# Exponents of the last round written into the query slots, and three moves beside it, in a recurrent-memory attention kernel

## The chip, the cores and the metric

The kernel runs on one core of a Trainium2 chip. The metric is the device time of one execution in microseconds, and the median over several runs is quoted. Beside these runs one execution was recorded by the hardware profiler; its rows, in microseconds from the start of the span, are what the durations below come from.

## The reference

Four layers are applied in turn to x, 2048 tokens of 640 numbers: A, B, A, B, each on the layer norm of x and added to it.

```python
def _A_ref(x, mem0, Wq, Wk, Wv, Wo, seg_len):     # seg_len 32, M 8, H 32, Dh 192
    ...
    for s in range(n_seg):                        # 64 segments
        xs = x[:, s * seg_len:(s + 1) * seg_len, :].copy()
        h = jnp.concatenate([mem, xs], axis=1)
        q = jnp.einsum('btd,dhe->bhte', h, Wq)
        k = jnp.einsum('btd,dhe->bhte', h, Wk)
        v = jnp.einsum('btd,dhe->bhte', h, Wv)
        scores = jnp.einsum('bhqe,bhke->bhqk', q, k) * scale
        scores = jnp.where(mask[None, None], scores, -1000000000.0)
        p = _softmax(scores, axis=-1)
        o = jnp.einsum('bhqk,bhke->bhqe', p, v)
        o = jnp.einsum('bhte,hed->btd', o, Wo)
        mem = o[:, :M, :].copy()
        outs.append(o[:, M:, :])
    return jnp.concatenate(outs, axis=1)

x = x + _A_ref(_layernorm(x, axis=-1), A_mem0, A_Wq, A_Wk, A_Wv, A_Wo, A_seg_len)
x = x + _B_ref(_layernorm(x, axis=-1), B_wqkv, B_w_phi, B_wo)      # linear attention with softmax features
x = x + _A_ref(_layernorm(x, axis=-1), A_mem0, A_Wq, A_Wk, A_Wv, A_Wo, A_seg_len)
x = x + _B_ref(_layernorm(x, axis=-1), B_wqkv, B_w_phi, B_wo)
```

In an A layer the first eight output rows of one segment are the memory that the next segment starts from, so its 64 segments follow one another.

## The kernel before

**Stages.** An A layer has a preparation (`A_pre`), which computes what does not depend on the memory, and a chain (`A_chain`) over the 64 segments. The last eight tokens of a segment, called tails, don't depend on the memory: their keys, queries and values are made in the preparation, put into device memory (`kqb_d`, `vb_d`) and fetched back by POOL during the chain. The other 32 rows of a segment (8 of memory, 24 of tokens) are projected in the chain from `hT`. What the tails' queries attend to is kept in `otb_d` for all segments and multiplied by the output matrix only at the head of the following B layer (`post_steps`): there `fetch` brings 16 segments of it back, `spread` copies them into the order that the matmul takes (eight copies of 128x768, two for each round r; the letters v and s choose DVE or ACT), and `multiply` makes 48 pairs of matmuls into two PSUM tiles, `kv` and `ps_post`.

**One segment.** The 32 heads are taken in four rounds n = 0..3 of eight; L is 3, the last. Everything in the chain is issued in the order in which the program is written (`tc.manual_schedule()`), each engine taking its own instructions in that order. `QK` is one tile, of which `KT` holds the turned keys and `QT` the turned queries, eight slots of 80 columns each: columns 0 to 63 for rows of the chain, 64 to 79 for tails, which POOL copies in (L1069). In each round PE makes `ps_qk_q`, `ps_qk_k` and `ps_v` (L1092), ACT copies q and k out of PSUM into `raws` (L1107), and DVE transposes them into `QT` and `KT` (L1112). `scores` (L1129) multiplies them, ACT takes the exponents (L1218) into a tile `E`, of which there is one. `v_rows` copies the values out of `ps_v` into `Vp`, one half on ACT (L1119), the other on DVE (L1121). `attend` multiplies `E` with `Vp` for rows (L1142) and, as `attend_tails`, for tails (L1155). DVE takes the reciprocal of the sums of exponents (`weigh_rows`: L1162 in rounds 0 to 2, L1166, one for each G, in the last), ACT multiplies by it (`scaled`, L1172), DVE transposes the result (`turn`: L1285 in rounds 0 and 2, L1293 in 1 and 3), and `wo_round` (L1198) multiplies it by the output matrix, adding up over the rounds in a PSUM tile `ps_w`.

**The end of a segment.** The products of rounds 0 to 2 with the output matrix fill places where PE would wait. `outs` lists those not yet made as 14 steps of four matmuls, two steps of round 0, six of round 1, six of round 2, and `output_steps(k)` makes the next k. Two are made in round 2 (`STEPS[0]`), five after the last scores (`STEPS[1]`), the rest after the last `attend`. So in the last round, before the change, the order on the engines is:

- DVE: keys transposed (L1112, two halves), `turn` of round 2 (L1285), the values' half (L1121), `hx_transpose`, which fills `hT` of the next segment from its tokens (L1043), the reciprocals (L1166), `turn` of round 3 (L1293), and after the last `wo_round` the turn of `ps_w` (L1371) and the new memory rows (L1373).
- ACT: the scaling of round 2 (L1172, twice), the values' half (L1119), the exponents (L1218), the scaling of round 3 (L1172, twice).
- PE: values (L1092), scores (L1129), the tails of round 2 (L1155, they read the `E` of round 2), five output steps, `attend` (L1142, L1155), the rest of the output steps, `wo_round` of round 3, four matmuls into `ps_idle` (L1205), then the next segment's queries.

At the start of the next segment `keep_rows` (L1051, L1054) reads the finished `ps_w` on ACT and DVE. `ps_w` has two buffers, which take turns from segment to segment; the other chain pools have one bank for each tag. Behind the last segment come, in this order: the first `spread_tails` (before the last `wo_round`; two rounds on DVE, two on ACT, "vvss"), `weigh_tail` (L1178), `tail_rows` (L1183), the turn of it (L1187), `keep_rows`.

**PSUM at the border.** Pools hand out the eight banks in the order in which tiles first ask for them: `ps_qk_q` and `ps_qk_k` take the first two, `ps_w` the next two, then `ps_v`, `ps_s`, `ps_o`, `ps_t`. The B layer behind it takes three for `kv`, the fourth for its side tile, which is `ps_post` at first, and four for the rest.

Of the kernel before, what the change touches and what calls it, by code (L numbers as in the profile page):

```python
# [8 lines left out]
P = 128  # L9
BF16 = mybir.dt.bfloat16  # L10
# [16 lines left out]
VH = 194  # L27
# [1 line left out]
PACE = {("Q", 0): 0, ("K", 0): 1, ("V", 0): 3, ("Q", 1): 4, ("K", 1): 4, ("V", 1): 3, ("Q", 2): 1, ("K", 2): 0, ("V", 2): 0,  # L29
        ("Q", 3): 0, ("K", 3): 0}  # L30

STEPS = (2, 5)

LATE = 64512
ARENA = 201728
# [90 lines left out]
class Kernel:  # L126
# [876 lines left out]
    def A_chain(self, xn_dram, at_dram, li, load_slot, piece, late_wo, load_both, wo, low):  # L1003
# [3 lines left out]
        with tc.tile_pool(name=f"A{li}_ch", reuse_waits="tile", bufs=1) as sp, \  # L1007
# [126 lines left out]

            def attend(E, n):
                O = [pop.tile([P, 512], F32, name="ps_o", tag="o0")] * 2
                if n == NR - 1:
                    O[1] = pop.tile([P, 512], F32, name="ps_o1", tag="v")
                V = Vs[n % 2]
                for G in range(2) if n < NR - 1 else (1, 0):  # L1140
                    for h in range(4):
                        nc.tensor.matmul(O[G][32 * h:32 * h + 32, VH * G:VH * G + 193], lhsT=E[0:80, 80 * h + 32 * G:80 * h + 32 * G + 32],  # L1142
                                         rhs=V[0:80, VH * h:VH * h + 193], start=True, stop=True, tile_position=(0, 32 * h),
                                         skip_group_check=True)
                if n != 2:
                    attend_tails(E, n)
                return O

            def attend_tails(E, n):
                V = Vs[n % 2]  # L1150
                if n % 2 == 0:
                    pair[0] = pop.tile([P, 512], F32, name="ps_t", tag="o1")
                q, m = (48, 32) if n % 2 == 0 else (64, 16)
                for h in range(4):
                    nc.tensor.matmul(pair[0][32 * h:32 * h + m, 0:193], lhsT=E[0:80, 80 * h + q:80 * h + q + m],  # L1155
                                     rhs=V[0:80, VH * h:VH * h + 193], start=True, stop=True, tile_position=(0, 32 * h),
                                     skip_group_check=True)

# [54 lines left out]
            def weigh(E_before=None):  # L1213
                S = scores()
                if E_before is not None:
                    attend_tails(E_before, 2)
                E = sp.tile([P, 320], BF16, name="E", tag="E")
                nc.scalar.activation(out=E[0:80, 0:320], in_=S[0:80, 0:320], func=ACT.Exp, scale=scale)  # L1218
                return E

            turns = [(s, r) for s in range(NSEG) for r in rounds(s)]

# [17 lines left out]
            kqs.append(load_kqb(0, rounds(0)[3]))  # L1240
            load_rows(1)
            for s in range(NSEG):
                W = pop.tile([P, 512], F32, name="ps_w", tag="w", bufs=2)
                order = rounds(s)
                L = NR - 1

# [31 lines left out]
                def turn(n, osc):  # L1278
                    if n in (0, 2):
                        if n == 0:  # L1280
                            rows = ots[0].rearrange("p (c j) -> p c j", j=64)
                        else:
                            rows = raw_of["K"][:, 0:384].rearrange("p (c j) -> p c j", j=64)
                        OTs.append([rows[:, 3 * G:3 * G + 3, :] for G in range(2)])
                        nc.vector.transpose(out=rows, in_=osc.rearrange("p (c j) -> p c j", j=64))  # L1285
                        return
                    if n == L:
                        OTs.append([KT[:, 3 * G:3 * G + 3, 0:64] for G in range(2)])
                    else:
                        OTs.append([ots[1][:, 192 * G:192 * G + 192].rearrange("p (c j) -> p c j", j=64) for G in range(2)])  # L1290
                    parts = osc if n == L else [osc[:, 192 * G:192 * G + 192] for G in range(2)]
                    for v, part in list(zip(OTs[n], parts))[::-1 if n == L else 1]:
                        nc.vector.transpose(out=v, in_=part.rearrange("p (c j) -> p c j", j=64))  # L1293
# [8 lines left out]
                for n in range(L):  # L1302
# [33 lines left out]
                    osc = raw_of["Q"][:, 0:384]  # L1336
                    for G in range(2):
                        scaled(osc[:, 192 * G:192 * G + 192], O, rc, G, "s")
                    turn(n, osc)
                    v_rows(pv, n + 1, "sv")  # L1340
                    if n == 1:
                        otr = tail_rows(rct, "OTh")
                E = weigh(E)
# [13 lines left out]
                turn(L, oscs)  # L1357
                output_steps(len(outs))
                if s == NSEG - 1:
                    self.first_tails = tails, [self.spread_tails(0, tails[0], low, "vvss")]  # L1360
                if s + 1 < NSEG:
                    if s + 2 < NSEG:
                        load_rows(s + 2)
# [13 lines left out]
            store_tail(turn_tail(tail_rows(rct, "OTh"), ots[1][:, 0:192]), NSEG - 1, order[L])  # L1377
            keep_rows(W_done)
            store_rows(NSEG - 1)

    def keep_tails(self, tb, low):
        self.kept_tails.append(self.fetch_tails(tb, low))
# [8 lines left out]
    def spread_tails(self, tb, ot, low, engines="vsvs"):  # L1391
        o = 7680 + 12288 * (tb % 2)
        ow = low[:, o + 6144:o + 12288].rearrange("p (r j s x) -> p r j s x", r=4, j=6, x=16)
        for r in range(4):
            for b in range(2):
                at = 192 * (r // 2) + (0 if (r + b) % 2 else 16)
                o = ow[:, r, :, b:16:2, :]
                i = ot[:, b:16:2, at:at + 16]
                i = ap3(i, [list(i.ap[0]), [32, 6], *[list(d) for d in i.ap[1:]]])
                self.ev.copy(out=o, in_=i, eng=engines[r])  # L1400
        return ow
# [64 lines left out]
```

## Time and profile before

| | |
|---|---|
| median of 3 runs | 3265.13 us (3263.06 to 3274.89) |
| the profiled execution, its own time | 3262.61 us |
| its span | 3260.9 us |
| busy in it | PE 3093.0 us (95%), DVE 2207.3 (68%), ACT 1882.7 (58%), POOL 1411.0 (43%) |
| chain of layer 0, of layer 2 | about 175 to 1374 us, about 1813 to 3003 us |
| from the first L1166 of a segment to that of the next | 17.93 us at the least, 18.31 us in the median |
| idle of PE's weight loads before L1142, until ACT E L1218 | 45.6 us, 125 times |
| idle of ACT before L1218, until PE ps_t L1155 | 27.7 us, 128 times |
| idle of DVE before L1121, until ACT Vp L1119 | 23.0 us, 38 times |

The span is the recorded part of the execution; 1.7 us of the profiled execution's time lie around it. A row such as "L1121 DVE CAST Vp<-ps_v 64x384" is read as: line 1121, on DVE, a copy from the PSUM tile `ps_v` to `Vp`, of 64 partitions by 384 elements. In rows in order of time the first number is the start, the second the busy time, "xN" the number of instructions that the row merges, and square brackets hold the time that the engine idled before and what ended it. PEld is TensorE's weight load, PE the matmul.

### The profile page before, as it was taken

Reading aid. Unit: us, or ns where it says so; the run is one execution under the profiler, and the core shown is the slowest. Engines: PE = TensorE matmul, PEld = TensorE weight load, DVE = VectorE, ACT = ScalarE, POOL = GpSimd, SP = SyncE. Lnnn points to the kernel's source line nnn. Section 1 sums busy time; section 2 is a strip of 40 time slices with the busy share of each in tenths; the row PEclk is TensorE's granted clock in tenths of the full one; section 3 lists DMA queues with packets and bytes.
Section 4 is the critical chain, followed back from the end, with each engine's and each line's share of the span. In section 5 each row is a group of like instructions: output and inputs, shape, how many; then the busy total and the mean of one; then the engine's idle time right before and its main releaser. Section 6 shows DMA issues by size and latency. Waiting matters only on the chain.

```text
span 3260.9 us, 140891 instructions
## 1 busy us (share of the span) xinstructions
PE 3093.0 (95%) x59424; PEld 1976.8 (61%) x59730; DVE 2207.3 (68%) x5457; ACT 1882.7 (58%) x4481; POOL 1411.0 (43%) x2920
## 2 busy tenths in 40 slices
PE   9989999999999999899999899999999999998999
PEld 7756666666666666555367566666666666665553
DVE  5557777777777777656643577777777777776565
ACT  3346666666666666546433466666666666666453
POOL 3345555555555554430122355555555555554300
PEclk9999999999999999999999999999999999999999
DMA  8977777777777777840385777777777777778300
GB/s 301 379 274 261 239 252 250 237 256 248 244 260 235 258 248 244 278 155 1 112 318 192 241 239 264 245 256 242 254 253 244 260 238 253 249 245 284 129 1 33
DMA packets 325018, 747.58 MB, mean 229 GB/s; under 512 B 65818, under 2 KB 100274, under 8 KB 321314
## 3 DMA queue, kind: packets, MB, share of 16 engines
q1 hardware_dynamic: 254850, 638.55, 56.3%
q0 software_dynamic: 67616, 86.77, 9.6%
q10 hardware_dynamic: 1920, 13.24, 1.0%
q8 instruction: 469, 7.68, 1.0%
q14 instruction: 163, 1.34, 0.1%
HBM read 668.80 MB, written 77.03 MB: 229 GB/s over the span
## 4 chain that ended last, share of the span: by engine, by line
PE 75%; DMA 11%; DVE 7%; ACT 3%; issue 3%; POOL 0%; SPq 0%; PEld 0%; DVEq 0%; POOLq 0%; ACTq 0%
PE ps_qk_q L1092 12%; PE ps_qk_k L1092 12%; PE ps_v L1092 11%; PE ps_w L1198 10%; PE ps_pre L960 6%; PE ps_s L1129 5%; DMA arena<-in_A_Wv_dram 5%; DMA Vp<-vb 3%; PE ps_pre L989 3%; PE ps_o L1142 3%; PE kv L1421 2%; DMA arena<-wo_rows 2%; DVE raws L1371 2%; PE ps_wo L444 2%; DVE hT L1373 2%
## 5 line engine op out<-in xcount | busy, mean ns | idle before, releaser
L1092 PEld LDWEIGHTS <-hT 128*32 128x32 bf16 x30720 | 790.0, 97 | 422.7 <-issue 40.3
L1112 DVE STREAM_TRANSPOSE QK<-raws 128x512 bf16<-128x512 bf16 (+1 forms) x1152 | 730.4, 642 | 205.5 <-ACT raws L1107 171.4
L1092 PE MATMUL ps_qk_q<-arena,hT 128*32 128x384 bf16 x10240 | 508.5, 327 | 36.3 <-DVE hT L1373 30.4
L1092 PE MATMUL ps_qk_k<-arena,hT 128*32 128x384 bf16 x10240 | 510.0, 328 | 5.4 <-DMA arena<-in_A_Wk_dram 2.3
L1069 POOL COPY QK<-kqb 64x192 bf16<-64x192 bf16 x1024 | 350.4, 342 | 376.7 <-PE ps_s L1129 340.1
L1107 ACT ACTIVATE raws<-ps_qk_k 128x512 bf16<-128x512 f32 (+1 forms) x640 | 313.5, 510 | 253.5 <-PE ps_qk_k L1092 253.5
L1092 PE MATMUL ps_v<-arena,hT 128*32 128x384 bf16 x8192 | 436.0, 327 | 14.3 <-issue 6.8
L1073 POOL DMA_DIRECT2D Vp<-vb x512 | 257.6, 503 | 417.0 <-PE ps_t L1155 252.3
L1172 ACT ACTIVATE raws<-ps_o,rc 128x192 bf16<-128x192 f32 x1024 | 373.7, 420 | 109.8 <-DVE rc L1166 107.5
L1107 ACT ACTIVATE raws<-ps_qk_q 128x512 bf16<-128x512 f32 x512 | 305.7, 597 | 162.5 <-PE ps_qk_q L1092 151.2
L1062 POOL DMA_DIRECT2D kqb<-kqb x512 | 290.6, 568 | 70.9 <-POOL QK L1069 50.2
L1198 PE MATMUL ps_w<-arena,under 128*32 128x320 bf16 x6144 | 306.2, 300 | 11.9 <-issue 8.8
L1121 DVE CAST Vp<-ps_v 64x384 bf16<-64x384 f32 x512 | 286.3, 559 | 38.3 <-ACT Vp L1119 23.0
L1129 PEld LDWEIGHTS <-QK 128*80 128x80 bf16 x4096 | 195.5, 120 | 160.8 <-issue 156.6
L1119 ACT ACTIVATE Vp<-ps_v 64x384 bf16<-64x384 f32 x512 | 246.4, 481 | 55.6 <-PE ps_v L1092 54.8
L1129 PE MATMUL ps_s<-QK 128*80 128x80 bf16 x4096 | 256.4, 210 | 3.8 <-POOL QK L1069 2.8
L1218 ACT ACTIVATE E<-ps_s 80x320 bf16<-80x320 f32 x512 | 217.6, 425 | 30.7 <-PE ps_t L1155 27.7
L1051 ACT ACTIVATE wh<-ps_w 64x160 f32<-64x160 f32 x256 | 76.6, 299 | 266.1 <-DVE raws L1371 256.2
L1058 POOL DMA_DIRECT2D attn<-under x128 | 91.6, 716 | 294.2 <-DVE under L1054 291.3
L960 PEld LDWEIGHTS <-arena 128*128 128x128 bf16 x1920 | 188.4, 98 | 31.6 <-DVE next_xT L97 4.6
L97 DVE CAST arena<-ps_pre 128x512 bf16<-128x512 f32 (+1 forms) x160 | 102.2, 646 | 143.2 <-PE ps_pre L960 96.2
L1142 PE MATMUL ps_o<-Vp,E 80*32 80x193 bf16 x4096 | 179.9, 248 | 18.1 <-DMA Vp<-vb 7.4
(159 smaller groups left out, 4580.7 us busy)
## 6 DMA issues: line engine op xcount, KB each, us to landing
arena<-wo_rows SPq DMA_DIRECT2D x560, 320.0 KB, 5.5
arena<-in_A_Wq_dram SPq DMA_DIRECT2D x427, 384.0 KB, 4.2
arena<-in_A_Wk_dram SPq DMA_DIRECT2D x298, 384.0 KB, 4.7
arena<-in_A_Wv_dram SPq DMA_DIRECT2D x290, 384.0 KB, 6.0
kqb<-kqb POOLq DMA_DIRECT2D x512, 48.0 KB, 4.9
vb<-arena POOLq DMA_DIRECT2D x128, 97.0 KB, 6.1
Vp<-vb POOLq DMA_DIRECT2D x512, 24.2 KB, 4.0
kqb<-arena SPq DMA_DIRECT2D x8, 1536.0 KB, 9.7
```

The lines of the kernel that those rows point to most:

```text
L960: nc.tensor.matmul(ps[:, T * i:T * i + T], lhsT=w[b][:, P * c:P * c + P], rhs=xBT[:, b, :], start=(b == 0), stop=(b == KC - 1))
L1062: nc.gpsimd.dma_start(out=kqb[:], in_=self.kqb_d[r, :, s, :])
L1069: nc.gpsimd.tensor_copy(out=o, in_=kqb[h, :].rearrange("p (x c q) -> p x c q", c=3, q=16))
L1073: nc.gpsimd.dma_start(out=Vs[n % 2][64:80, :], in_=self.vb_d[s, r].rearrange("g t f -> (g t) f"))
L1092: last = nc.tensor.matmul(o, lhsT=hT[:, b, :], rhs=rhs, start=(i == 0), stop=(i == KC - 1), tile_position=(0, 32 * g), skip_group_check=True)
L1107: nc.scalar.activation(out=raw[:, c], in_=ps[:, c], func=ACT.Copy)
L1112: nc.vector.transpose(out=o, in_=i)
L1121: nc.vector.tensor_copy(out=o, in_=i)
L1129: nc.tensor.matmul(S[0:80, c0:c0 + 80], lhsT=KT[:, 4 * x + c, :], rhs=QT[:, 4 * x + c, :], start=(c % 2 == 0), stop=(c % 2 == 1), skip_gro ...
L1142: nc.tensor.matmul(O[G][32 * h:32 * h + 32, VH * G:VH * G + 193], lhsT=E[0:80, 80 * h + 32 * G:80 * h + 32 * G + 32], rhs=V[0:80, VH * h:V ...
L1172: nc.scalar.activation(out=out, in_=i, func=ACT.Copy, scale=rc[G])
L1198: step = nc.tensor.matmul(W[q:q + 32, 0:320], lhsT=OT[i // 6][:, i % 6 // 2, 32 * (i % 2):32 * (i % 2) + 32], rhs=rhs, start=(first and i ...
```

## The change

Four things change. The first three act in every segment of both chains or at their ends; the layers B are untouched.

1. `weigh` with an argument, which is the call of the last round, writes the exponents into `QT`, in two instructions: those of rows and the first 64 queries into slots 0 to 3, those of the last 16 queries of each head into slot 4. `attend` and `attend_tails` take a function that gives the columns. Rounds 0 to 2 use `E` as before.
2. In the third round (n = 2) `turn` is called behind `v_rows` instead of ahead of it, and `STEPS[1]` is 6 instead of 5, so that all steps ahead of the last `attend` are of round 1.
3. `ps_w` has one buffer instead of two.
4. The first `spread_tails` is split: its DVE half stays where it was, its ACT half is called at the very end of `A_chain`, behind `keep_rows` and `store_rows`.

```diff
-STEPS = (2, 5)
+STEPS = (2, 6)
...
-                        nc.tensor.matmul(O[G][32 * h:32 * h + 32, VH * G:VH * G + 193], lhsT=E[0:80, 80 * h + 32 * G:80 * h + 32 * G + 32],
+                        nc.tensor.matmul(O[G][32 * h:32 * h + 32, VH * G:VH * G + 193], lhsT=E(h, 32 * G, 32),
...
-                    nc.tensor.matmul(pair[0][32 * h:32 * h + m, 0:193], lhsT=E[0:80, 80 * h + q:80 * h + q + m],
+                    nc.tensor.matmul(pair[0][32 * h:32 * h + m, 0:193], lhsT=E(h, q, m),
...
                 S = scores()
                 if E_before is not None:
                     attend_tails(E_before, 2)
-                E = sp.tile([P, 320], BF16, name="E", tag="E")
-                nc.scalar.activation(out=E[0:80, 0:320], in_=S[0:80, 0:320], func=ACT.Exp, scale=scale)
-                return E
+                if E_before is None:
+                    E = sp.tile([P, 320], BF16, name="E", tag="E")
+                    nc.scalar.activation(out=E[0:80, 0:320], in_=S[0:80, 0:320], func=ACT.Exp, scale=scale)
+                    return lambda h, q, m: E[0:80, 80 * h + q:80 * h + q + m]
+                rows = S[0:80, 0:320].rearrange("p (h q) -> p h q", h=4)
+                nc.scalar.activation(out=QT[0:80, 0:4, 0:64], in_=rows[:, :, 0:64], func=ACT.Exp, scale=scale)
+                nc.scalar.activation(out=QT[0:80, 4, 0:64].rearrange("p (h q) -> p h q", h=4), in_=rows[:, :, 64:80],
+                                     func=ACT.Exp, scale=scale)
+                return lambda h, q, m: QT[0:80, 4, 16 * h + q - 64:16 * h + q - 64 + m] if q >= 64 else QT[0:80, h, q:q + m]
...
-                W = pop.tile([P, 512], F32, name="ps_w", tag="w", bufs=2)
+                W = pop.tile([P, 512], F32, name="ps_w", tag="w")
...
-                    turn(n, osc)
+                    if n < L - 1:
+                        turn(n, osc)
                     v_rows(pv, n + 1, "sv")
+                    if n == L - 1:
+                        turn(n, osc)
...
                 if s == NSEG - 1:
-                    self.first_tails = tails, [self.spread_tails(0, tails[0], low, "vvss")]
+                    self.spread_tails(0, tails[0], low, "vv")
...
             store_rows(NSEG - 1)
+            self.first_tails = tails, [self.spread_tails(0, tails[0], low, "  ss")]
...
         for r in range(4):
+            if engines[r:r + 1] in ("", " "):
+                continue
             for b in range(2):
```

## The prediction

> **What bounds it.** I read the page's chain of waits first, then the waits of each engine, then the rows in order of time around the end of one segment and around the border to the last layer.
>
> ```profile
> PE 75%; DMA 11%; DVE 7%; ACT 3%; issue 3%; POOL 0%; SPq 0%; PEld 0%; DVEq 0%; POOLq 0%; ACTq 0%
> ```
>
> PE carries the chain, DVE 7% of it. DVE's part lies at the ends of the segments, where the change works. An undisturbed segment of layer 0 (DVE, ACT and weight loads, three answers of the same stretch, put one behind the other):
>
> ```profile
> 625.70 0.77 DVE L1112 STREAM_TRANSPOSE QK<-raws 128x256 bf16<-128x256 bf16 x2
> 626.59 0.58 DVE L1285 STREAM_TRANSPOSE raws<-raws 128x384 bf16<-128x384 bf16 x1
> 627.20 0.56 DVE L1121 CAST Vp<-ps_v 64x384 bf16<-64x384 f32 x1
> 627.68 0.35 DVE L1043 STREAM_TRANSPOSE hT<-xr 128x160 bf16<-128x160 bf16 x1
> 628.13 0.25 DVE L1166 RECIPROCAL rc<-ps_o 128x1 f32<-128x1 f32 x2
> ...
> 626.53 0.48 ACT L1119 ACTIVATE Vp<-ps_v 64x384 bf16<-64x384 f32 x1
> 627.22 0.43 ACT L1218 ACTIVATE E<-ps_s 80x320 bf16<-80x320 f32 x1 [0.20 <-PE ps_t L1155]
> 628.39 0.42 ACT L1172 ACTIVATE raws<-ps_o,rc 128x192 bf16<-128x192 f32 x1 [0.74 <-DVE rc L1166]
> ...
> 626.85 0.60 PEld L1198 LDWEIGHTS <-under 128*32 128x32 bf16 x20
> 627.70 0.23 PEld L1142 LDWEIGHTS <-E 80*32 80x32 bf16 x8 [0.25 <-ACT E L1218]
> 628.06 0.80 PEld L1198 LDWEIGHTS <-raws 128*32 128x32 bf16 x24
> 629.27 0.41 PEld L1198 LDWEIGHTS <-QK 128*32 128x32 bf16 x16 [0.41 <-DVE QK L1293]
> ```
>
> From the reciprocals on, one thing waits for the next: ACT idles 0.74 for L1166, and PE, its filling work done at 628.86, idles 0.41 for the transposes behind it. So whatever moves L1166 moves the segment's end, and with it the next segment. Ahead of L1166, DVE goes through turn, cast and L1043 with no idle of note, and the 0.25 that PE idles for E is what parts 1 and 2 are about. The cast has a second condition, seen in a segment whose values came late:
>
> ```profile
> 609.21 0.56 DVE L1121 CAST Vp<-ps_v 64x384 bf16<-64x384 f32 x1 [0.53 <-ACT Vp L1119]
> ```
>
> ACT's half had ended at 609.18; DVE's starts 0.03 later. The smallest distance between the two over all 512 pairs is 0.03, so DVE's half waits for ACT's half.
>
> **Part 1, exponents.** The wait that goes is L1218's for the tails of round 2: 27.7 us over 128, 0.22 each. The one instruction of 423 ns becomes two. Their forms aren't in the trace: 80x256 lies between 423 (80x320) and, below, 301 (64x160 on ACT is 299, L457's 128x128 301); the nearest row is
>
> ```profile
> L1107 ACT ACTIVATE raws<-ps_qk_k 128x256 bf16<-128x256 f32 x256 | 84.2, 381 | 52.9 <-PE ps_qk_k L1092 52.9
> ```
>
> so I take 380. The second, 80x64, lies between 0 and 300; the line through 381 (256) and 597 (512) gives 0.84 ns an element and 219. The second runs into ACT's idle of 0.74 ahead of L1172 and costs nothing; without that cover it would be 0.2 a segment. ACT's half of the values ends at 627.01, so E for rows would be there at 627.41 instead of 627.65.
>
> **Part 2, the turn.** DVE's cast starts at 627.01 + 0.03 = 627.04 instead of 627.20, DVE having idled from 626.47, and ends at 627.60. PE gets through six steps at 626.85 + 24 x 0.030 = 627.57, has E at 627.41 and V at 627.60, and can start `attend` near 627.66 instead of 627.82: 0.16 earlier. But what is late next is DVE's queue. The turn of 0.58, until now done while ACT cast its half, stands behind the cast, and L1043 and L1166 stand behind it. Starts follow each other by 0.48 from cast to transpose (627.20 to 627.68), 0.51 from one transpose to the next (0.58 less the overlap of 0.07 that the two halves of L1112 show, 0.77 against 2 x 0.424), 0.375 from L1043 to a read of PSUM (0.345 and the 0.03 that lie between L1285's end and the cast). Then L1166 starts at 627.04 + 0.48 + 0.51 + 0.375 = 628.41 instead of 628.13: 0.28 later, although its sums lie ready. In general it is 1.395 behind the end of ACT's half.
>
> I did this sum for all 128 segments from their own rows (end of L1119, start of L1166). Without the last segments of each chain, which have no L1043, 75 lose over 0.25, 23 less, and in 28 L1166 already came as late for another reason. PE idles for L1293 in 97 segments; those lose 21.8 us together. In the other 29 PE's own filling was late and covers the delay; four more matmuls ahead of `attend` cost up to 0.1 each there, 3 us. **Chain: +25 us**, bounds +8 (every other stall of the segment covers it) and +39 (126 times 0.31, nothing covered). The PE filling of round 2's sums starts at 628.16 instead of 628.06 and ends ahead of 629.5, so it is hidden.
>
> **Parts 3 and 4, the border.** Rows in order of time at the end of layer 2's chain:
>
> ```profile
> 3006.40 3.04 ACT L99 ACTIVATE arena<-arena 128x768 bf16<-128x768 bf16 x4 [5.32 <-DMA arena<-wo_rows]
> 3006.42 1.17 DVE L97 COPY arena<-arena 128x768 bf16<-128x768 bf16 x4 [4.93 <-DMA arena<-wo_rows]
> 3007.10 0.10 PEld L1421 LDWEIGHTS <-arena 128*128 128x128 bf16 x1 [4.01 <-DVE arena L97]
> 3009.35 0.40 ACT L1183 ACTIVATE otr<-ps_t,rct 128x192 bf16<-128x192 f32 x1
> 3009.77 0.61 ACT L1051 ACTIVATE wh<-ps_w 64x160 f32<-64x160 f32 x2
> 3010.41 0.65 DVE L1054 TENSOR_TENSOR under<-ps_w,wh 64x160 bf16<-64x160 f32 x2 [0.26 <-ACT wh L1051]
> 3011.20 0.26 PE L1422 MATMUL ps_post<-arena 128*128 128x128 bf16 x1 [8.12 <-DVE under L1054]
> ```
>
> PE has its first operands at 3007.10, but `ps_post` lies in the fourth bank, which the last segment's `ps_w` (its second buffer) holds until L1054. With one buffer `ps_w` has the third bank, the fourth is `ps_v`'s, last read by L1172 at 3001. So PE starts at 3007.1: 4.1 us earlier. If the bank were the same as before, part 4 alone would bring L1183 from 3009.35 to 3007.66, 1.7 us. ACT's four copies, 3.04, would then stand at about 3008.7 to 3011.8; they are wanted by the 25th pair of matmuls, no earlier than 3007.1 + 24 x 0.27 = 3013.6. The next fetch, which needs their place, was issued at 3012.84 anyway. The border of layer 0 shows the same: 1377.51 against 1381.62. Behind both, PE's products set the pace. **Border: -8.2 us**, bounds -3.4 and -12 (below). One buffer costs nothing in the chain: the new sum starts in round 1, microseconds behind L1054.
>
> PE's clock in the stretches shown: 0.88 from 3003 to 3007, 0.50 from 3007 to 3016; in layer 0 1.00 from 1373 to 1377 and 0.61 from 1377 to 1381. So an idle of 3.5 to 4 us may or may not slow the first products; six to nine pairs at 0.53 instead of 0.27 are 1.6 and 2.4 us, and the bound of -12 has both. The Trainium skill, "TensorE: Matmul & The Clock Gate", section "What's actually happening", says that after an idle window of about 3.4 us the clock halves and that the window runs freely; the rows agree, and by it the gain may fall on either side. I count none.
>
> **Sum.** 25 - 8 = +17 us on the profiled execution's 3262.6 (span 3260.9): 3280. The median of the runs stands 2.5 above it, so 3282.
>
> **Rivals.**
>
> *The delay is covered (20%).* Segments take 17.93 at best and 18.31 in the median, the rest is waits for weights and for nothing shown; if a later end gives loads time, the +25 shrinks to +8 and below, and the border's gain shows. For it: DMA has 11% of the chain. Against it: between 611 and 615 the DMA engines are 5 to 38% busy, the old loads are through by then. 3265 + 8 - 8 = 3265, down to 3257.
>
> *Nothing is covered (10%).* Every segment loses 0.31, +39, and the border gives little: up to 3304.
>
> *DVE is not in the way (4%), faster.* If the two halves of the values could be read at once, DVE's cast would start at 626.53, the turn end at 627.59, L1043 at 627.87, and L1166 be PE's alone: `attend` at 627.62, L1166 0.31 behind it, 0.2 earlier than before, 97 x 0.2 = 19 us. 3265 - 19 - 8 = 3238. It decides where the cast starts under 0.03 behind ACT's half. Against it stand the 38 waits. The Trainium skill, "PSUM — Partial Sum Buffer", section "PSUM bank collisions raise a hardware error", holds that engines may read different quadrants of one bank together, and the halves are partitions 0 to 63 and 64 to 127. The trace doesn't agree: the program orders them, with 23.0 us of waits.
>
> *The tails' copies get between (4%).* POOL copies tails into columns 64 to 79 of the same tile between exponents and `attend`; if these were ordered, `attend` would wait (L1069 runs from 627.97 for 0.74) from 627.66 to 628.71 + 0.05, L1166 come at 629.07, 0.94 x 126 = 118 us, 3375. Against it: at 617.33 POOL's copy and at 617.54 DVE's transpose into the same slots run together.
>
> **Chances.** Forecast 62%, its own range 3272 to 3294; with the rivals the range is 3257 to 3300, which leaves out the two 4% cases and the ends of others. A measurement tells 0.5%, 16 us, from no change: below 3249 or above 3281.5. The forecast falls 0.33 above and 0.29 inside; with covered 0.16 inside and 0.04 below, the others as said: faster 0.08, same 0.45, slower 0.47.
>
> **What would show it.** Right: L1166 about 1.4 behind the end of L1119 and with no wait for `ps_o`; L1218 no longer waiting for `ps_t`; `attend` 0.1 to 0.2 earlier against the scores; PE's idle for L1293 up from 0.41 to 0.7; `ps_post` starting right behind the first copies. Wrong: L1166 still waiting for `ps_o`, or a cast beside ACT's.

## The result, and the profile after

| | before | after |
|---|---|---|
| median of 20 runs each, same chips | 3268.23 us (3259.60 to 3276.76) | 3280.64 us (3261.46 to 3290.06) |
| after to before | | 1.0033, 95% interval 1.0021 to 1.0045 |
| span of the profiled execution | 3260.9 us | 3278.5 us |
| chain of layer 0, of layer 2 | 1202.9, 1194.0 | 1213.7, 1209.0 |
| border behind each | 8.0, 8.5 | 4.2, 4.1 |

The kernel became slower, by 0.33% or 10.8 us (6.9 to 14.7). The ratio need not be the quotient of the two medians, which lie 12.4 us apart. The chain is counted here from the first `ps_qk_q` of a layer to the start of its last `ps_idle` matmul, the border from there to the first `ps_post`. From the profiled execution of before to that of after, the chains grew by 25.8 us and the borders shrank by 8.1; the stretch of layer B and the preparation behind it took 427.1 us before and 429.5 after.

The chain of waits of the changed kernel, with PE's share down from 75% and DVE's up from 7%:

```profile
PE 70%; DVE 10%; DMA 10%; ACT 5%; issue 4%; POOL 1%; SPq 0%; DVEq 0%; POOLq 0%; ACTq 0%
```

The end of a segment of layer 0 after, in three answers of one stretch (DVE, ACT, weight loads). The turn of round 2 is now L1291, that of the last round L1299, the exponents L1222 and L1223:

```profile
666.57 0.56 DVE L1121 CAST Vp<-ps_v 64x384 bf16<-64x384 f32 x1 [1.88 <-ACT Vp L1119]
667.05 0.56 DVE L1291 STREAM_TRANSPOSE raws<-raws 128x384 bf16<-128x384 bf16 x1
667.55 0.31 DVE L1043 STREAM_TRANSPOSE hT<-xr 128x160 bf16<-128x160 bf16 x1
667.89 0.23 DVE L1166 RECIPROCAL rc<-ps_o 128x1 f32<-128x1 f32 x2
...
666.05 0.49 ACT L1119 ACTIVATE Vp<-ps_v 64x384 bf16<-64x384 f32 x1 [1.27 <-PE ps_v L1092]
666.47 0.38 ACT L1222 ACTIVATE QK<-ps_s 80x256 bf16<-80x256 f32 x1
666.75 0.21 ACT L1223 ACTIVATE QK<-ps_s 80x64 bf16<-80x64 f32 x1
668.15 0.73 ACT L1172 ACTIVATE raws<-ps_o,rc 128x192 bf16<-128x192 f32 x2 [1.19 <-DVE rc L1166]
...
667.14 0.24 PEld L1142 LDWEIGHTS <-QK 80*32 80x32 bf16 x8
667.67 0.66 PEld L1198 LDWEIGHTS <-raws 128*32 128x32 bf16 x24 [0.20 <-DVE raws L1291]
669.04 0.66 PEld L1198 LDWEIGHTS <-QK 128*32 128x32 bf16 x24 [0.70 <-DVE QK L1299]
```

DVE has idled 1.88 when its cast starts 0.03 behind the end of ACT's half (666.54), and then it never pauses: 0.48 to the turn, 0.50 to L1043, 0.34 to L1166. L1166 starts 1.35 behind ACT's half. Its sums were ready earlier: `attend` ended at about 667.6. ACT idles 1.19 for L1166 (0.74 in the segment shown of before), PE 0.70 for the last turn (0.41 before).

The same over all segments, in the waits of each engine (engine and line, what it waited for, us in total, times, the longest), first after:

```profile
ACT raws L1172 <- DVE rc L1166: 169.9, 128, 3.8
...
DVE Vp L1121 <- ACT Vp L1119: 105.2, 128, 2.5
...
PEld L1198 <- DVE QK L1299: 66.2, 105, 0.8
...
DVE rc L1166 <- PE ps_o L1142: 20.2, 27, 2.7
```

Before, the same four were:

```profile
ACT raws L1172 <- DVE rc L1166: 107.5, 131, 1.8
...
PEld L1198 <- DVE QK L1293: 39.2, 97, 0.4
...
DVE rc L1166 <- PE ps_o L1142: 31.0, 82, 1.5
...
DVE Vp L1121 <- ACT Vp L1119: 23.0, 38, 1.4
```

Three of them grew: the cast now stands behind ACT's half every time, ACT stands longer behind L1166, PE behind the turn. Not all of ACT's growth is loss: its exponents also end earlier, and in the kernel with the turn undone (below), which loses nothing, its row is 134.2 us. The row of L1166 shrank: it seldom waits for its sums. L1218's wait for `ps_t`, 27.7 us before, has no row any more.

The border of layer 0 after, in order of time:

```profile
1386.16 1.17 DVE L97 COPY arena<-arena 128x768 bf16<-128x768 bf16 x4 [4.54 <-DMA arena<-wo_rows]
...
1386.84 0.10 PEld L1433 LDWEIGHTS <-arena 128*128 128x128 bf16 x1 [3.62 <-DVE arena L97]
...
1387.07 0.22 PE L1434 MATMUL ps_post<-arena 128*128 128x128 bf16 x1 [3.86 <-DVE arena L97]
...
1387.13 0.38 PE L1433 MATMUL kv<-arena 128*128 128x512 bf16 x1
...
1387.40 0.62 PE L1433 MATMUL kv<-arena 128*128 128x512 bf16 x1
...
1387.44 0.42 ACT L1183 ACTIVATE otr<-ps_t,rct 128x192 bf16<-128x192 f32 x1 [6.23 <-DVE rct L1178]
```

`ps_post` starts right behind the first copies instead of 8 us into the border, and L1183 no longer stands behind ACT's four copies. After an idle of 3.86 the first pair ran at 0.38 a `kv` product, the next ones at 0.62: the clock fell 0.3 us after PE had resumed (granted 1.00 from 1387.07 to 1387.40, then 0.50 to 1390.50). The Trainium skill, "TensorE: Matmul & The Clock Gate", section "What's actually happening", has a window of about 3.4 us that runs freely, after which the clock is halved; this idle, just above it, still met the halving, in agreement.

### The profile page after: what moved, and what is told of

Read it like the earlier page. It is cut to its first block, busy times and chain, and to the rows that moved or that the text cites. A ratio compares the mean times of both kernels' runs of the same rounds, so it can differ in the third digit from the quotient of the medians.

```text
span 3278.5 us, 140636 instructions
## 1 busy us (share of the span) xinstructions
PE 3095.2 (94%) x59424; PEld 1976.0 (60%) x59730; DVE 2191.1 (67%) x5457; ACT 1886.3 (58%) x4609; POOL 1417.5 (43%) x2920
## 4 chain that ended last, share of the span: by engine, by line
PE 70%; DVE 10%; DMA 10%; ACT 5%; issue 4%; POOL 1%; SPq 0%; DVEq 0%; POOLq 0%; ACTq 0%
PE ps_qk_q L1092 12%; PE ps_qk_k L1092 12%; PE ps_v L1092 11%; PE ps_w L1198 8%; PE ps_s L1129 5%; PE ps_pre L960 4%; DMA arena<-in_A_Wv_dram 4%; PE kv L1433 2%; ACT raws L1172 2%; PE ps_o L1142 2%; DVE raws L1380 2%; PE ps_pre L989 2%; DMA Vp<-vb 2%; PE ps_wo L444 2%; DVE hT L1382 2%
## 5 line engine op out<-in xcount | busy, mean ns | idle before, releaser
L1073 POOL DMA_DIRECT2D Vp<-vb x512 | 258.6, 505 | 430.1 <-PE ps_t L1155 264.7
L1121 DVE CAST Vp<-ps_v 64x384 bf16<-64x384 f32 x512 | 286.2, 559 | 117.2 <-ACT Vp L1119 105.2
L1198 PE MATMUL ps_w<-arena,under 128*32 128x320 bf16 x6144 | 283.4, 300 | 11.7 <-issue 8.1
L1119 ACT ACTIVATE Vp<-ps_v 64x384 bf16<-64x384 f32 x512 | 247.5, 483 | 55.9 <-PE ps_v L1092 54.6
L99 ACT ACTIVATE arena<-ps_pre 128x512 bf16<-128x512 f32 (+1 forms) x160 | 92.6, 596 | 160.7 <-PE ps_pre L960 106.7
L1198 PEld LDWEIGHTS <-under 128*32 128x32 bf16 x6144 | 147.0, 96 | 45.6 <-issue 16.4
```

The costliest lines, as they stand in the source:

```text
L1073: nc.gpsimd.dma_start(out=Vs[n % 2][64:80, :], in_=self.vb_d[s, r].rearrange("g t f -> (g t) f"))
L1119: nc.scalar.activation(out=o, in_=i, func=ACT.Copy)
L1121: nc.vector.tensor_copy(out=o, in_=i)
L1198: step = nc.tensor.matmul(W[q:q + 32, 0:320], lhsT=OT[i // 6][:, i % 6 // 2, 32 * (i % 2):32 * (i % 2) + 32], rhs=rhs, start=(first and i ...
```

## The experiments

Each ratio below is of a kernel to the kernel before, from runs on the same chip, with its 95% interval; like the ratio above it need not be the quotient of the two medians. The kernels were not all run on one chip, so two of them are compared here by their ratios, not by their times. Two measures from the traces stand beside them. The **shortest segments** are the 5th percentile of the 126 times from the first L1166 of a segment to that of the next: 17.93 us before, 18.17 after. The **distance** is from the end of ACT's half of the values to the start of L1166, in the median: 1.11 before, 1.35 after. Segments and distances are from one profile of each kernel. The theory to be tested is that DVE's queue (turn and L1043 ahead of L1166) makes the loss. The rivals are that the two exponent instructions, the sixth output step, or the border's edits make it.

### The turn alone, undone and done

Undone in the changed kernel:

```diff
-STEPS = (2, 6)
+STEPS = (2, 5)
...
-                    if n < L - 1:
-                        turn(n, osc)
+                    turn(n, osc)
                     v_rows(pv, n + 1, "sv")
-                    if n == L - 1:
-                        turn(n, osc)
```

> The changed kernel with part 2 undone: the turn of round 2 ahead of the cast again, five steps ahead of the last attend; exponents in the query slots, one ps_w buffer and the split spread stay. Theory (DVE's queue carries the loss: turn and L1043 ahead of the last reciprocals): the chains lose their +25.8 us (10.8 and 15.0 in the profiles) and come back to about 1203 + 1194 = 2397 us or up to 6 us below, since attend is still held by the cast at its old place; L1166 in the median 1.10 behind the end of ACT's half as before the change; the border keeps -8; time 0.997 to 0.998 of the kernel before. Rival (the two instructions for exponents or their place in the query slots carry the loss): the chains stay near 2423 us, time about 1.003.

Measured: 0.9970 (0.9953 to 0.9987), medians 3257.31 and 3269.94 us. Shortest segments 17.93, distance 1.11; borders 4.2 and 4.7. So without part 2 the rest of the change is a gain of 0.3%.

Done alone, in the kernel before (the same lines the other way round, nothing else):

> The kernel before with part 2 alone: the turn of round 2 behind the cast and six steps ahead of attend; exponents in E, two ps_w buffers, the spread as it was. Theory (DVE's queue): L1166 again 1.34 to 1.36 behind the end of ACT's half in the median although attend is now held by E (0.78 or so), shortest segments 18.17 us, borders 8 us; time 1.005 to 1.009 of the kernel before. Rival (the loss needs the exponents in the query slots): 17.93 and 1.000.

Measured: 1.0059 (1.0041 to 1.0077), shortest segments 18.17, distance 1.35, borders 8.0 and 8.9. The whole loss is in part 2, and it doesn't need the exponents of part 1.

### Which part of the queue: L1043 moved behind the last turn

This leaves the turn where the change put it, but takes L1043 out of the queue ahead of L1166:

```diff
-                if s + 1 < NSEG:
-                    hT = new_hT()
-                    hx_transpose(hT)
                 O = attend(E, L)
...
                 turn(L, oscs)
+                if s + 1 < NSEG:
+                    hT = new_hT()
+                    hx_transpose(hT)
```

> The changed kernel with one move: the transpose L1043 that fills hT from the next tokens is issued behind the turn of round 3 instead of ahead of the last attend. Theory (DVE's queue): L1166 starts 0.03 behind the end of the turn of round 2, that is 0.03 + 0.48 + 0.58 + 0.03 = 1.12 behind the end of ACT's half in the median instead of 1.35; the chains shrink by about 97 x 0.25 = 24 us to about 2399; time 0.997 to 0.998 of the kernel before. Rival (exponents or PE's sixth step carry the loss): L1043 is no matter, chains near 2423 us, about 1.003. If L1043 in its new place comes in the way of the turn of ps_w, the chains stay long and L1371's counterpart starts later behind the last wo_round than 0.05.

Measured: 0.9990 (0.9973 to 1.0006). A segment's DVE rows in this kernel:

```profile
629.78 0.56 DVE L1121 CAST Vp<-ps_v 64x384 bf16<-64x384 f32 x1 [0.95 <-ACT Vp L1119]
...
630.26 0.56 DVE L1291 STREAM_TRANSPOSE raws<-raws 128x384 bf16<-128x384 bf16 x1
...
630.86 0.23 DVE L1166 RECIPROCAL rc<-ps_o 128x1 f32<-128x1 f32 x2
...
632.19 0.31 DVE L1043 STREAM_TRANSPOSE hT<-xr 128x160 bf16<-128x160 bf16 x1
```

L1166 follows the turn at 0.60; the distance is 1.11 and the shortest segments are 17.93 again. One transpose of 0.31 off the queue takes the loss away at the shortest segments, and 0.43% of the time (from 1.0033 to 0.9990), with the exponents, the sixth step and the turn behind the cast all still there. That is the theory's case; the rivals would have kept the loss. Whether this kernel differs from the one with the turn undone (0.9970) isn't told apart: the intervals overlap. Its profile doesn't settle it: the chains took 2414 us in it instead of the 2399 expected, since the segments lay 99 us in sum above their shortest there, against 76 in the profile of the changed kernel.

### Half a turn behind the cast

On top of the last kernel, the turn of round 2 is cut in two, one half ahead of the values and one behind:

```diff
+                def turn_half(osc, G):
...
+                    nc.vector.transpose(out=rows[:, 3 * G:3 * G + 3, :],
+                                        in_=osc[:, 192 * G:192 * G + 192].rearrange("p (c j) -> p c j", j=64))
...
+                    else:
+                        turn_half(osc, 0)
                     v_rows(pv, n + 1, "sv")
                     if n == L - 1:
-                        turn(n, osc)
+                        turn_half(osc, 1)
```

> The kernel of the run before with the turn of round 2 cut in two: its first half (three of six slots) ahead of the cast, its second behind it. Theory: the first half fills DVE's wait for ACT's half (627.04 less 626.47 = 0.57 idle, a half takes 0.34), the cast starts 0.03 behind ACT's half, the second half ends 0.48 + 0.34 = 0.82 behind the cast's start and L1166 finds its sums just ready: 0.74 + 0.31 = 1.05 or less behind the end of ACT's half, as attend now starts 0.74 behind it. Against the kernel before (1.11) that is 0.06 to 0.15 a segment over 97, 6 to 15 us, and the border's 8: time 0.993 to 0.996 of the kernel before. Rival: attend or the exponents hold L1166 and the halves cost more than the whole: 0.998 or above.

Measured: 0.9974 (0.9959 to 0.9989). The distance fell to 1.05 and the shortest segments to 17.87, but the time isn't below that of the turn undone, and the ratio lies above the range expected. 0.06 x 126 = 8 us at the bottom of the segments didn't come out at the end. With these intervals 8 us are hard to tell, but it is a first hint that something else holds many segments.

### The exponents alone

Part 1 put into the kernel before:

```diff
+                rows = S[0:80, 0:320].rearrange("p (h q) -> p h q", h=4)
+                nc.scalar.activation(out=QT[0:80, 0:4, 0:64], in_=rows[:, :, 0:64], func=ACT.Exp, scale=scale)
+                nc.scalar.activation(out=QT[0:80, 4, 0:64].rearrange("p (h q) -> p h q", h=4), in_=rows[:, :, 64:80],
+                                     func=ACT.Exp, scale=scale)
```

> The kernel before with part 1 alone: exponents of the last round in the query slots. Theory (attend is held by the cast as much as by the exponents, and the cast keeps its place): attend starts at most 0.05 earlier behind ACT's half (0.64 to 0.79 as in the run with the turn ahead, against 0.69 to 0.80), the shortest segments stay at 17.93 us or go to 17.89; time 0.998 to 1.000. Rival (the wait of 0.22 for the tails is worth itself): shortest segments 17.71, 0.993. Rival (the split exponents cost): shortest segments longer than 17.93.

Measured: 0.9994 (0.9977 to 1.0012), shortest segments 17.93, distance 1.11, and the last `attend` 0.80 behind ACT's half, as before. Part 1 is worth nothing by itself and costs nothing: the wait that it removes was not the last one.

### The border: both parts, and each alone

Parts 3 and 4 in the kernel before:

```diff
-                W = pop.tile([P, 512], F32, name="ps_w", tag="w", bufs=2)
+                W = pop.tile([P, 512], F32, name="ps_w", tag="w")
...
-                    self.first_tails = tails, [self.spread_tails(0, tails[0], low, "vvss")]
+                    self.spread_tails(0, tails[0], low, "vv")
...
             store_rows(NSEG - 1)
+            self.first_tails = tails, [self.spread_tails(0, tails[0], low, "  ss")]
```

> The kernel before with parts 3 and 4 alone: one ps_w buffer and the split spread. Theory: the chains stay at 2397 us give or take the 5 us by which stalls differ, the two borders (last ps_idle to first ps_post) go from 8.0 and 8.5 to 4.2 and 4.1 us; time 0.9975 of the kernel before (-8 us). Rival (one ps_w buffer makes the next segment's sum wait and costs in the chain): L1198 of round 1 waits for L1054, chains longer, time 1.000 or above.

Measured: 0.9985 (0.9966 to 1.0003), borders 4.5 and 4.7. In the trace the borders are 7.3 us shorter (8.0 and 8.5 before); the ratio's interval holds the 0.9975 expected, without proving it. The profile fell on the slowest of this kernel's 12 runs (3281.0 us): its chains took 2416 us, 19 more than expected, though the shortest segments are 17.93 as before and no row has L1198 waiting for L1054, which was the rival.

The one buffer alone (the first two lines of the diff):

> The kernel before with part 3 alone: one ps_w buffer. Theory (the fourth bank carries the border's gain): ps_post starts 4.1 us after the last ps_idle in both borders as in the changed kernel, while L1183 still starts behind ACT's four copies (3.0 us after them); the shortest segments stay at 17.93. Rival (part 4 carries it): ps_post still 8 us behind the last ps_idle.

In its one profile the borders took 4.9 and 4.7. That of layer 0:

```profile
1377.20 1.17 DVE L97 COPY arena<-arena 128x768 bf16<-128x768 bf16 x4 [5.19 <-DMA arena<-wo_rows]
...
1378.11 0.22 PE L1422 MATMUL ps_post<-arena 128*128 128x128 bf16 x1 [4.51 <-DVE arena L97]
...
1380.13 0.40 ACT L1183 ACTIVATE otr<-ps_t,rct 128x192 bf16<-128x192 f32 x1
```

`ps_post` starts 0.91 behind the first of DVE's copies, exactly as in the changed kernel (1386.16 to 1387.07), although L1183 still stands behind ACT's copies. The 0.7 by which the border is longer lie ahead of the copies. These start 0.12 behind the landing of the tails' rows from `otb_d` in both kernels (1377.08 here, 1386.04 there), although the row names another DMA. The split of the copies alone (the rest of the diff):

> The kernel before with part 4 alone: the ACT half of the first spread behind keep_rows, two ps_w buffers. Theory: L1183 starts right behind L1178 (0.05 to 0.2) instead of 1.85 later, L1054 ends 1.7 us earlier and ps_post with it: 6.2 to 6.8 us behind the last ps_idle instead of 8.0 and 8.5, against 4.7 to 4.9 with one ps_w buffer alone. Rival: 8 us as before.

In its one profile the borders took 6.3 and 6.6. That of layer 2:

```profile
3007.68 0.42 ACT L1183 ACTIVATE otr<-ps_t,rct 128x192 bf16<-128x192 f32 x1 [6.32 <-DVE rct L1178]
...
3008.77 0.65 DVE L1054 TENSOR_TENSOR under<-ps_w,wh 64x160 bf16<-64x160 f32 x2 [0.26 <-ACT wh L1051]
...
3009.56 0.27 PE L1425 MATMUL ps_post<-arena 128*128 128x128 bf16 x1 [2.08 <-DVE under L1054]
```

With two buffers `ps_post` still waits for L1054, which the split only brings forward. So the bank is what parts 3 and 4 are about. Counted from the first copy, `ps_post` comes 4.79 later in the kernel before, 3.16 with part 4 alone, and 0.91 to 1.09 with part 3, whether part 4 is there or not. Part 4 alone is worth 1.6; beside part 3 it adds nothing that shows.

### Two banks for the values

If L1121 stands behind L1119 only because both read one PSUM tile, two tiles would let it start beside it. On top of the kernel with L1043 late, in the bank that part 3 freed, and with five steps ahead again:

```diff
-STEPS = (2, 6)
+STEPS = (2, 5)
...
-                        o = ps[32 * g:32 * g + 32, 0:384]
+                        o = ps[g // 2][32 * g:32 * g + 32, 0:384] if m == "V" else None
...
-                    i = pv[64 * x:64 * x + 64, 0:384].rearrange("p (e f) -> p e f", e=2)
+                    i = pv[x][64 * x:64 * x + 64, 0:384].rearrange("p (e f) -> p e f", e=2)
...
-                    return pop.tile([P, 512], F32, name="ps_v", tag="v")
+                    return [pop.tile([P, 512], F32, name=f"ps_v{x}", tag="vx"[0:1 + x]) for x in range(2)]
```

> The changed kernel with L1043 behind the turn of round 3, five steps ahead of attend, and the values' two halves in two PSUM tiles, in the bank that the one ps_w buffer set free. Theory (the order of the two casts comes from the common PSUM tile, and DVE's place in it holds attend): DVE's cast starts beside ACT's, attend is held by PE and the exponents alone and starts about 0.45 to 0.50 behind the end of ACT's half instead of 0.74, L1166 0.8 behind it; shortest segments 17.6 to 17.7 us; if stalls don't grow, 126 x 0.27 = 34 us and the border's 8 less: 0.987 of the kernel before; if weights set the pace where PE waits less, half of it, 0.992. Rival (the casts wait for something else): cast still 0.03 behind ACT's half, shortest segments 17.93, 0.998.

Measured: 0.9970 (0.9956 to 0.9984). A segment of it in order of time:

```profile
639.96 0.48 ACT L1119 ACTIVATE Vp<-ps_v 64x384 bf16<-64x384 f32 x1
640.00 0.56 DVE L1121 CAST Vp<-ps_v 64x384 bf16<-64x384 f32 x1
...
640.48 0.56 DVE L1291 STREAM_TRANSPOSE raws<-raws 128x384 bf16<-128x384 bf16 x1
640.67 0.21 ACT L1223 ACTIVATE QK<-ps_s 80x64 bf16<-80x64 f32 x1
...
641.18 0.15 PEld L1142 LDWEIGHTS <-QK 80*32 80x32 bf16 x8 [0.29 <-ACT QK L1223]
...
641.52 0.25 DVE L1166 RECIPROCAL rc<-ps_o 128x1 f32<-128x1 f32 x2 [0.48 <-PE ps_o L1142]
```

The cast runs beside ACT's half, the turn ends at 641.04, and DVE is out of the way: L1166 now waits 0.48 for its sums. The shortest segments fall to 17.73. Yet the time is that of the turn undone, not the 0.987 to 0.992 expected, and the distance in the median is 1.11 as before. The reason is in the row of L1142: it is put down to L1223, but that had ended at 640.88, 0.30 earlier. What came at 641.07 is the landing of the tails' values, fetched by L1073 at 636.00 into `Vp`; in no segment does the last `attend` start earlier than 0.13 behind this landing. It starts within 0.15 of it in 72 of 128 segments here, in 48 of the changed kernel and in 49 of the kernel before. The windows of this stretch (us; busy time of PE, its weight loads, DVE, ACT, POOL with instructions; clock; DMA share; GB/s) show what the 24 KB, which take 5 us, run beside:

```profile
637.00:639.00 2.00, 2.00 (x56) 1.35 (x52) 1.90 (x6) 1.57 (x6) 0.74 (x3) 1.00 1.01 356
639.00:641.00 2.00, 2.00 (x56) 1.26 (x48) 1.83 (x5) 1.88 (x7) 1.23 (x3) 1.00 1.04 390
641.00:643.00 2.00, 1.92 (x60) 1.25 (x56) 1.05 (x6) 0.73 (x2) 1.84 (x5) 1.00 0.36 121
```

The DMA engines are full with weights until the landing. That this holds the segments was the next thing to test.

### Without the fetch

Left out of the last kernel, and of the kernel before:

```diff
+                if n == NR - 1 and s > 0:
+                    return
                 nc.gpsimd.dma_start(out=Vs[n % 2][64:80, :], in_=self.vb_d[s, r].rearrange("g t f -> (g t) f"))
```

> The kernel with two banks for values, without the fetch of the tails' values of the last round from the second segment on (these rows of Vp keep what round 1 had, so the sums of that round are not the reference's). In the kernel with the fetch the last attend starts never earlier than 0.13 behind the fetch's landing, and 0.13 to 0.15 behind it in 72 of 128 segments. Theory (landing holds attend there): attend comes 0.61 to 0.65 behind the end of ACT's half in the median instead of 0.79, L1166 0.93 instead of 1.11; the shortest segments stay at 17.73, and the sum of the segments shrinks by 10 to 20 us: 0.992 to 0.994 of the kernel before. Rival (chance meeting; PE's own order holds attend): median stays at 0.79, time 0.997.

Measured: 0.9876 (0.9857 to 0.9895). The distance is 0.93 and the shortest segments stay at 17.73: the fetch lengthens the others. The gain, 0.94% on the last kernel (each against the kernel before on its own chip), is more than expected.

> The kernel before, without the fetch of the tails' values of the last round from the second segment on (those rows are not the reference's). There attend starts within 0.15 of the landing in 49 of 128 segments. Theory (in most other segments exponents and cast hold it just as long): attend 0.69 to 0.71 behind the end of ACT's half in the median instead of 0.80, the shortest segments still 17.93, time 0.997 to 0.999 of the kernel before, the rest of the stalls being weights and what the trace names issue. Rival (the fetch doesn't matter): 0.80, 1.000.

Measured: 0.9936 (0.9918 to 0.9953), more than expected too. The median start of the last `attend` behind ACT's half stayed at 0.79; its 90th percentile fell from 1.18 to 1.05. So in the kernel before the fetch decides in the late segments only, elsewhere the values' cast does, and expecting the median to move was wrong. Both runs also spare POOL the issue and the DMA engines 126 x 24 KB, so they bound what the landing costs from above.

### The fetch kept, issued by ACT

```diff
-                nc.gpsimd.dma_start(out=Vs[n % 2][64:80, :], in_=self.vb_d[s, r].rearrange("g t f -> (g t) f"))
+                (nc.scalar if n == NR - 1 and s > 0 else nc.gpsimd).dma_start(out=Vs[n % 2][64:80, :], in_=self.vb_d[s, r].rearrange("g t f -> (g t) f"))
```

> The kernel with two banks for values, with the fetch of the tails' values of the last round issued by ACT, behind the copy of round 2's keys and ahead of its scaling, instead of by POOL. Theory (landing holds the last attend in 72 segments): ACT is free for it about 0.4 before POOL has issued it (604.16 against 604.57 in the kernel before) and the weights' queue is another one, so attend comes 0.62 to 0.70 behind the end of ACT's half in the median instead of 0.79; but an issue on ACT takes 0.31 to 0.44 in the profile of the kernel before, and what is behind it on ACT (scaling, values' half, queries' copy) comes later by up to that in every segment: shortest segments 17.8 to 18.0 instead of 17.73. Together 0.993 to 1.000 of the kernel before; under 0.997 the landing weighs more, above it ACT's queue.

Measured: 0.9909 (0.9893 to 0.9926), medians 3239.48 and 3268.34 us. This kernel leaves nothing out, and it is quicker than both the kernel before and the changed one. The distance falls from 1.11 to 0.93, and 126 x 0.18 = 23 us is about what the ratio gained on the kernel with two banks (0.61%, 20 us). The shortest segments stay at 17.73; that the issue on ACT would lengthen them to 17.8 or more was wrong. Its issue, in order of time:

```profile
636.64 0.60 ACT L1107 ACTIVATE raws<-ps_qk_k 128x512 bf16<-128x512 f32 x1 [0.94 <-PE ps_qk_k L1092]
...
636.92 0.31 ACTq L1073 DMA_DIRECT2D Vp<-vb  x1
...
637.34 0.73 ACT L1172 ACTIVATE raws<-ps_o,rc 128x192 bf16<-128x192 f32 x2
```

The issue runs on ACT's sequencer while the engine still copies, and costs ACT about 0.1 (637.24 to 637.34). It starts 0.03 behind the tails' product that frees the buffer (its PE row ends at 636.89), 0.05 in the median; POOL's, in the kernel with two banks, started 0.31 behind (635.69 to 636.00), the median too, and took 0.50. The landing comes 0.27 behind ACT's half in the median instead of 0.64, and holds `attend` in 18 segments instead of 72. The waits of PE ahead of `attend` in the kernel with two banks:

```profile
PEld L1142 <- ACT QK L1223: 22.4, 51, 0.9
...
PE ps_o L1142 <- DMA Vp<-vb: 13.8, 30, 1.1
```

And with the issue on ACT:

```profile
PEld L1142 <- ACT QK L1223: 4.0, 11, 0.8
...
PE ps_o L1142 <- DMA Vp<-vb: 1.7, 5, 0.5
```

Nothing was done to L1223 between the two, so most of its 22.4 us were the landing's under another name. Between this kernel and the one without the fetch 0.33% remain; whether that is landings still late or the traffic itself stays open. A third buffer for the values, with which the fetch could be issued a round earlier, was not tried.

## Why the prediction was right, and where not

**Direction and mechanism: right.** DVE's queue behind the cast is the cause: part 2 alone gives the loss, L1043 taken out of the queue removes it at the shortest segments and most of it in the time, and the rest of the change is a gain. That the median lies 1.4 us under the forecast is partly luck: the kernel before stands at 3268.2 over 20 runs, 3.1 above the median that the forecast started from, and the step from it is +10.8 (6.9 to 14.7) instead of +17.

**L1166 behind ACT's half: right, a little too late.** Forecast 1.395, measured 1.35 in the median, with 92 of 128 segments between 1.30 and 1.38 (8 before). The terms were 0.03, 0.48, 0.51 and 0.375; in the rows above they are 0.03, 0.48, 0.50 and 0.34. The last was too high: L1043 itself took 0.31 instead of 0.35.

**The chain's +25 us: right in the two profiles (10.8 + 15.0), high by the runs.** By the ratios, part 2 costs 0.63% or 20.6 us in the changed kernel (1.0033 against 0.9970) and 0.59% or 19 us in the kernel before (13 to 25). That interval alone doesn't exclude the 25. The step of the whole change does, if the borders gave back the 8.1 of the profiles: 10.8 + 8.1 = 18.9, with 15 to 23 as bounds. So this is the term of the sum that was mis-sized. The distance accounts for most of it, as a sum and not as an experiment: 0.045 less in each of the 97 segments that I counted as losing is 4.4 us. The cover was about as reckoned: the shortest segments lost 0.24, over 126 that is 30 us, and a third of it doesn't show in the time. But I had looked for the cover in PE's own filling alone and overlooked the landing of the tails' values, which held `attend` in 49 of 128 segments already before. How much of the third is the landing's was not tested: the turn's place was never varied without the fetch. The bound of +39 has 0.31 a segment, where the sum itself gives 0.28 in the median, or 36; the +8 has no working behind it. A single profile can't settle such a sum: what lies above the shortest segments (the 126 times less 126 times the shortest) was anything from 84 to 102 us in the profiles of those kernels whose shortest segments are 17.93 and that keep the fetch.

**`attend` 0.16 earlier: wrong in size.** Its start behind ACT's half moved from 0.80 to 0.74 in the median. I had PE start 0.06 behind the end of DVE's cast; it was 0.15 in the median, which takes over half of the 0.16. In the sum it changed nothing, since L1166 no longer waits for `attend`.

**The exponents: right.** Forecast 380 and 219 ns, hidden; the groups after (count, us in total, mean ns, idle before):

```profile
L1222 ACT ACTIVATE QK<-ps_s 80x256 bf16<-80x256 f32 x128 | 48.8, 381 | 1.7 <-PE ps_s L1129 1.5
L1223 ACT ACTIVATE QK<-ps_s 80x64 bf16<-80x64 f32 x128 | 27.0, 211 | 0.0
```

**The border's -8.2: right** (-8.1), with the bank as the reason and part 4 alone at 1.6 where 1.7 was reckoned. The first pairs of products followed each other by up to 0.53 instead of 0.27: 6 and 9 of them before, 6 and 5 after. In the profiles of the other kernels it was 4 to 10, behind borders of 4 us as behind those of 8, so counting no gain from the clock was right.

**DVE not in the way: rightly put aside**, but the case with two tiles shows what decides it: the order of L1119 and L1121 comes from the tile or the bank that they share, which that run separated together. In two banks they run side by side. Whether the chip would let them read different partitions of one bank together, as the Trainium skill says ("PSUM — Partial Sum Buffer", section "PSUM bank collisions raise a hardware error"), no run here shows, since the program always orders them there; the 23.0 us of waits are this order and say nothing of the chip.

**The tails' copies between: didn't happen**; `attend` came earlier, not a microsecond later.

The net of the runs, +0.33%, is what the parts add up to: +0.59 for part 2, -0.15 for the border, -0.06 for the exponents make +0.38, well within their intervals.

## What to carry to other kernels

When an instruction moves within an engine's order, sum up the whole queue between its new place and the next thing that another engine waits for: here a wait of 27.7 us in the table went away and gained nothing, while 0.58 of transpose pushed behind a cast cost 0.6% of the time. After each improvement ask which input of the held instruction comes last now, the DMA landings included, since a wait may be put down to a producer that had ended long before. And a small fetch that must land at a point of a serial chain is worth issuing from the engine that can do so first.

## What had not been expected of the hardware

The 24 KB fetch took 4.3 to 6.8 us from issue to landing, 5.25 in the median, beside a weight stream that filled the DMA engines (shares of 0.91 to 1.04 in the windows from 631 to 641). The fetches of the other rounds, of the same size, show that it is the company they keep: in the profile of the kernel before, those of rounds 0 to 3 took 2.9, 2.1, 4.8 and 5.2 in the median, while the DMA engines were busy for 0.34, 0.23, 0.95 and 0.99 of that time. Issued by ACT, and then through another DMA queue, the fetch of the last round took 5.14. The Trainium skill, "DMA: Bandwidth & Descriptors", section "Issuing engines are not separate DMA queues", says that issuing from another engine saves only the time of initiating; the runs agree. From the issue's start to the landing there are 0.11 less, and the issue itself is 0.19 shorter; the start comes 0.26 earlier. Together that is the 0.37 by which the landing moved against ACT's half. In a chain that waits for the landing this was worth 0.6% (0.9970 to 0.9909).
